# Batch 0 of a polysketch attention + tanh-shrink FFN kernel: token-major on TensorE instead of transposed on VectorE

## The chip, the cores and the metric

The kernel runs on one core of one Trainium2 chip. The metric is the device time of one execution in microseconds (us). Before the change it is 114.63 us, the median of three runs (113.7, 114.63, 115.8).

## What is computed

Two stages are chained. The attention takes 4 batches of 4 heads, 1088 tokens of 32 numbers each:

```python
def phi(x):                                   # S1, S2: 8 x 32
    a = np.einsum('rd,bhsd->bhsr', S1, x)
    b = np.einsum('rd,bhsd->bhsr', S2, x)
    return np.einsum('bhsi,bhsj->bhsij', a, b).reshape(*x.shape[:-1], 64)
q_p, k_p = phi(q), phi(k)
kv  = np.einsum('bhsf,bhsd->bhfd', k_p, v)    # 64 x 32 per head
z   = np.sum(k_p, axis=2)
num = np.einsum('bhsf,bhfd->bhsd', q_p, kv)
den = np.einsum('bhsf,bhf->bhs', q_p, z)[..., None] + 1e-06
attn = num / den
```

Its result, as x with 4352 tokens (4 x 1088) of 128 numbers (4 heads x 32), goes through a feed-forward stage (FFN) of width 2048:

```python
h = x @ w_in              # 4352 x 2048
g = h - np.tanh(h)
out = g @ w_out           # 4352 x 128
```

The kernel computes h W_out as x (W_in W_out): one 128 x 128 product, kept as a high and a low bf16 part (`wch`, `wcl`). So the FFN is, per group of columns (tokens), 16 matmuls h = W_in^T x, 16 tanh with a minus sign, 16 matmuls with W_out, and two with `wch` and `wcl`.

## The kernel before, in words

All work is recorded as operations with inputs and outputs (`P.add`), and a planner in the kernel (`_Prog.schedule`, L151) decides at build time in what order each engine gets them, by costs written beside each operation (`_v`, `_a`, `_pe`, ...) and keys (due times). What runs on the chip are five fixed queues, one for each engine, with semaphore waits between them. Each engine works its queue strictly in order.

**Attention, per batch.** k and q are loaded with (head, time slot) on the partitions, VectorE turns them in 32 x 32 blocks (`kT` L583, `qT` L592), TensorE applies the sketch matrices (`ksk` L599/L610, `qsk` L724), and VectorE turns the result from PSUM back to token-major (`abk` L616, `abc` L729). For k, VectorE multiplies out the 64 products per token (`w`, L659, three pieces), and TensorE sums them against v (`kvmm`, L671); the result, values by features, is spread by ScalarE (`kvd`), turned on TensorE (`kvt`, L703) and copied (`kvb`). The denominator comes from a small Gram matrix of k's two sketches (`gram` L638, `scmm` L625). For q, VectorE forms the denominators (`m`, `den`, `rd`, `ap`, L741 to L749), the products (`qp`, L767) and turns them (`qpT`, L772); TensorE makes the numerators (`num`, L783, 32 x 32 tiles), and ScalarE and VectorE copy them to `xT` (x transposed, bf16, columns are tokens). Batch 0 is cut in pieces of 2, 3 and 4 blocks of 128 tokens, so that the FFN can start on the first 256 columns.

**FFN.** Ten groups of columns: 256, 384, 448, six of 512, and 192 (`GCOLS`). `h` is L877, the tanh `th` is L881 on ScalarE, the second product is L892 and L896. From group 7 on (`PAIRS`) a tanh covers two PSUM banks. VectorE turns each finished group (`ot`, L901), and SyncE writes it out (L911).

**Weights.** ScalarE and GpSimd cast W_in and W_out to bf16; TensorE turns W_in (`wit`, L845), ScalarE copies it (`wiT`), and 16 matmuls (`wc`, L855) make the 128 x 128 product.

**Loads.** All by SyncE's queue, in the order k0, the first 8 slots of q0, v0, one quarter of W_in, the rest of q0, the rest of W_in, W_out, then batches 1 to 3. A load waits (`after`) until no more than `CAP` = 1.4 MB of loads are under way. W_out is fetched in pieces of 512 bytes.

**Fillers.** While TensorE has nothing to do before the first W_out matmul, the planner puts in matmuls on zeros (L435).

Of the kernel before, what the change touches and what calls it, by code (L numbers as in the profile page):

```python
# [22 lines left out]
CAP = 1.4e6  # L23
# [68 lines left out]
class _Prog:  # L92
# [58 lines left out]
    def schedule(self, filler=None):  # L151
# [31 lines left out]
        while n < len(self.ops):  # L183
# [42 lines left out]
            occ, o.lat = o.engs[e]  # L226
            if o.dma:
                free[e] = t + occ
                wire = max(t + 1450.0, wire) + o.dma
                o.t1 = wire + (300.0 if o.key < -79000 else 2000.0)  # L230
            else:
                o.t1 = t + occ
                free[e] = o.t1
# [17 lines left out]
    def fill(self, filler, a, b):  # L251
        t = a
        while t + FILL[0] + FILL[1] < b:
            o = _Op()
            o.engs = {"tensor": (FILL[0], 215.0)}
            o.fn, o.key, o.dma, o.name, o.mode = filler[0], 0, 0, "fill", "128x128"
            o.deps, o.users, o.vals = {filler[1]: True}, [], []
            o.filler = True
            o.eng, o.t0, o.t1, o.lat = "tensor", t, t + FILL[0], 215.0
            o.inc, o.sem, o.waits, o.known = False, None, [], {}  # L260
            o.seq = len(self.order["tensor"])
            self.order["tensor"].append(o)
            t = o.t1
# [58 lines left out]
def _v(n):  # L322
    return {"vector": (n / 0.96 + 64.0, 143.0)}
# [22 lines left out]
def bass_polysketch_attn__then__act_tanh_shrink_kernel(  # L346
# [13 lines left out]
    def sb(name, shape, dtype=FP32):  # L360
        uid[0] += 1
        return nc.alloc_sbuf_tensor(f"{name}_{uid[0]}", shape, dtype).ap()
# [27 lines left out]
    kL = [sb("kL", [128, NC * 32]) for _ in range(B)]  # L390
    vL = [sb("vL", [128, H, NB * 32]) for _ in range(B)]
    qL = [sb("qL", [128, NC * 32]) for _ in range(B)]
    kT_p = pool("kT", 2, [128, 36 * 32])
    qTs = [sb("qT", [128, 36 * 32]) for _ in range(B)]
# [8 lines left out]
    rd_p = pool("rd", 2, [128, NB * H])  # L403
    kvd_p = pool("kvd", 2, [128, 256])
# [4 lines left out]
    NTH = 20  # L409
# [10 lines left out]
    mask4 = sbv("mask4", [128, H])  # L420
    sin = sbv("sin", [128, 2, 32])
# [16 lines left out]
    def pool_op(fn, r=(), w=(), n=100, key=-50000.0):  # L438
# [10 lines left out]
    P.add(_v(128), lambda e, n: e.tensor_reduce(  # L449
        out=mask2.ap[:, :], in_=ident.ap.rearrange("p (a e d) -> p e a d", a=2, e=2), op=ALU.add, axis=AX.XY),  # L450
        r=[ident], w=[mask2], key=-91000)
    for pl, f, val in ((kT_p, lambda a: a[:, 1088:1152], 0.0), 
                       (m_p, lambda a: a[:, :, 8:9], 1e-6)):
        for i, s_ in enumerate(pl.choices):
            o = pool_op(lambda e, n, a=f(s_[1][0]), val=val: e.memset(a, val), n=64, key=-49000)
            pl.seed(i, o)
    qpad = [sbv_ for sbv_ in (_Val(ap=qTs[b][:, 1088:1152]) for b in range(B))]
    for b in range(B):
        pool_op(lambda e, n, b=b: e.memset(qpad[b].ap, 0.0), w=[qpad[b]], n=64, key=-48500 + b)
    vvals = [[_Val(ap=vL[b][e * 64:(e + 1) * 64, :, :]) for e in range(2)] for b in range(B)]  # L460
    for b in range(B):
        P.add(_v(128), lambda e, n, b=b: e.memset(vL[b][64:128, :, 256:288], 0.0), w=[vvals[b][1]], key=-89000 + b)
# [3 lines left out]
    def load(key, o_, i_, w, nbytes, eng="sync", rate=330.0, cap=True):  # L466
        after = []
        if cap:
            left = CAP - nbytes
            for op, nb in reversed(loads):  # L470
                left -= nb
                if left < 0:
                    after = [op]
                    break
        op = P.add({eng: (450.0, 0.0)}, lambda e, n: e.dma_start(out=o_, in_=i_), w=w, key=key, dma=nbytes / rate,
                   after=after)
        loads.append((op, nbytes))
        return op

    for x, Sx in ((0, S1), (1, S2)):  # L480
        load(-99000 + x, sin.ap[:, x, :], Sx[None, :, :].to_broadcast([16, 8, 32]), [sin], 16384, "scalar")

    kvals = [[_Val(ap=kL[b].rearrange("p (r x) -> p r x", r=2)[:, :, e * 288:(544 if e else 288)]) for e in range(2)] for b in range(B)]
    qcut = {0: [0, 8, 34]}
    qvals = [[(a, z, _Val(ap=qL[b][:, a * 32:z * 32])) for a, z in zip(c[:-1], c[1:])]
             for b, c in ((b, qcut.get(b, [0, 34])) for b in range(B))]

    def load_k(key, b):
        src = k[b].rearrange("h (t r c) d -> (h t) r (c d)", r=2, c=17)
        if b == 0:  # L490
            for e in range(2):
                load(key + e, kvals[b][e].ap, src[:, :, e * 288:(544 if e else 288)], [kvals[b][e]], 128 * (256 if e else 288) * 8)
        else:
            load(key, kL[b][:, :], k[b].rearrange("h (t c) d -> (h t) (c d)", c=NC), kvals[b], 128 * 1088 * 4)

    def load_v(key, b):
        vs = v[b].rearrange("h (m x) d -> m h (x d)", x=17)
        for e in range(2):
            w_ = 256 if e else 288
            load(key + e, vL[b][e * 64:(e + 1) * 64, :, 0:w_], vs[:, :, e * 288:e * 288 + w_], [vvals[b][e]], 64 * w_ * 16)  # L500

    def load_q(key, b, i):
        a, z, val = qvals[b][i]
        src = q[b].rearrange("h (t c) d -> (h t) (c d)", c=NC)
        load(key, qL[b][:, a * 32:z * 32], src[:, a * 32:z * 32], [val], 128 * (z - a) * 128)
# [3 lines left out]
    wos = moe_w_out.rearrange("(jb ji) c -> ji jb c", jb=NJB, ji=128)  # L509
# [4 lines left out]
    def load_wo(key, i):  # L514
        load(key, wof[i].ap, wos[:, i * 4:(i + 1) * 4, :], [wof[i]], 128 * 2048)

    lk = iter(range(-90000, -80000, 10))
    load_k(next(lk), 0)
    load_q(next(lk), 0, 0)
    load_v(next(lk), 0)  # L520
    load_wi(next(lk), 0)
    load_q(next(lk), 0, 1)
# [4 lines left out]
    for b in range(1, B):  # L527
        load_k(next(lk), b)
        load_q(next(lk), b, 0)
        load_v(next(lk), b)  # L530

# [6 lines left out]
    def col_time(c):  # L538
# [14 lines left out]
        r=[stt, mask2], w=[wab], key=-85000)  # L553
    for w, z in zip(wqc, wqs):
        pool_op(lambda e, n, z=z: e.memset(z[:, 24:32], 0.0), w=[w], n=8, key=-48600)
        pool_op(lambda e, n, w=w: e.tensor_copy(
            w.ap.rearrange("p (x i) -> p x i", i=8), stt.ap.rearrange("p x (r i) -> p x r i", i=8)[:, :, 0, :]),
            r=[stt], w=[w], n=16, key=-48000)
# [19 lines left out]
    qTv = [[(NC, 36, qpad[b])] for b in range(B)]  # L578
# [9 lines left out]
    def q_transpose(b, i):  # L588
        a, z, val = qvals[b][i]
        tv = _Val(ap=qTs[b][:, a * 32:z * 32])  # L590
        qTv[b].append((a, z, tv))
        P.add(_v((z - a) * 32), lambda e, n: e.transpose(tv.ap, val.ap), r=[val], w=[tv], key=nk(), name=f"qT{b}.{i}")  # L592
# [28 lines left out]
    pg = [_Val(att1 if b else one(2)) for b in range(B)]  # L621
# [43 lines left out]
    pv = [_Val(att1 if b else one(1)) for b in range(B)]  # L665
# [44 lines left out]
    def q_in(b, s0, s1):  # L710
        return [v_ for (a, z, v_) in qTv[b] if a < s1 * 4 and z > s0 * 4]

    def qv4(b):
        return qTs[b].rearrange("p (k g t) -> p k g t", g=4, t=32)

    def q_sketch(b, s0, s1, abc):
# [10 lines left out]
        P.add(_pe(max(sn / 1.2, 55.0) * 2), sk, r=q_in(b, s0, s1) + [scv[b], wqc[b % 2]], w=pq, key=nk(), mode="32x32",  # L727
# [6 lines left out]
    def part(abc, x, c0, c1):  # L734
        return abc.ap.rearrange("p k h f -> p (k h) f")[:, c0 * 4:c1 * 4, x * 8:(x + 1) * 8]

    def q_divide(b, s0, s1, abc):
        nb = s1 - s0
# [3 lines left out]
            out=m_.ap[:, 0:nx, 0:8], in0=part(abc, 0, 0, nb), in1=part(abc, 2, 0, nb),  # L742
# [7 lines left out]
            out=aq.ap[:, 0:nx * 8].rearrange("p (x i) -> p x i", i=8), in0=part(abc, 0, 0, nb),  # L750
# [59 lines left out]

    def attention():
        bias[0] = -15000.0
        k_transposes(0)
        q_transpose(0, 0)
        k_sketch(0)
        gram(0)
        for p in range(3):
            k_outer(0, p)
        kv_mm(0)
        kv_tail(0)  # L820
        st = q_front(0, 0, 2)
        q_piece(0, 0, 0, 2, *st)
        bias[0] = 0.0
        q_transpose(0, 1)
        st = q_front(0, 2, 9)
        for b0, b1 in PIECES[0][1:]:
            q_piece(0, 2, b0, b1, *st)
        for b in range(1, B):
            k_side(b)
            q_transpose(b, 0)  # L830
            st = q_front(b, 0, 9)
            for b0, b1 in PIECES[b]:
                q_piece(b, 0, b0, b1, *st)

    def weights():
        for i in range(4):
            P.add({**_as(512), **_g(512)}, lambda e, n, i=i: copy(e, n, wi[i].ap[:, :], wif[i].ap), r=[wif[i]], w=[wi[i]], key=-1000 + i, name=f"wi{i}")
# [3 lines left out]
        for i in range(2):  # L841
            tp = _Val(bank_h)
            for j in range(8):
# [4 lines left out]
                    r=[wi[jb // 4], identb], w=[tp], key=T_FIRST + 1000 + 4000 * i, mode="128x128", name=f"wit{jb}")  # L848
            P.add(_a(1024), lambda e, n, tp=tp, i=i: copy(
                e, n, wiT[i].ap.rearrange("p j c -> p (j c)"), tp.ap.bitcast(BF16)[:, 0:1024]),  # L850
                r=[tp], w=[wiT[i]], key=T_FIRST + 1000 + 4000 * i, name=f"wiT{i}")
        wc = _Val(bank_h)
        prev = None
        for jb in range(16):
# [3 lines left out]
                key=T_FIRST + 6000, chain=prev, mode="128x128",  # L858
# [5 lines left out]
    def ffn(gi, c0, n_):  # L864
# [38 lines left out]
        ce = (c0 + n_) // 32  # L903
        while cb < ce:
# [86 lines left out]
```

## Time and profile before

| | |
|---|---|
| median of three runs | 114.63 us |
| the profiled execution's own time | 114.65 us |
| its span, first to last instruction | 112.6 us |
| TensorE (PE) busy | 100.3 us, 89% |
| ScalarE (ACT) busy | 79.9 us, 71% |
| VectorE (DVE) busy | 72.1 us, 64% |
| GpSimd (POOL) busy | 5.6 us, 5% |
| first FFN matmul, first tanh | 19.71 us, 20.03 us |
| last `num` of the attention | 82.04 us |
| last tanh ends | 108.46 us |

The profile's times are microseconds from the span's start. PEld is the loading of a matmul's stationary operand, which the profile lists apart from the matmul. A float32 matmul appears as two records for each instruction, a float32 transpose and a bf16 matmul as one. A matmul's listed duration contains its way through the array, so that the distance between starts says more on pace than the duration. "[1.22 <-DMA ...]" behind an instruction is how long its engine had been idle before it and what ended that.

### The profile page before, as it was taken

The page shows a single profiled execution, that of the slowest core. Times are in us where ns is not written, and L with a number is a line of the kernel's source. Part 1 is how long each engine was busy: PE and PEld are TensorE (multiplying, and loading weights), DVE is VectorE, ACT ScalarE, POOL GpSimd, SP SyncE. Part 2 cuts the span into 40 slices and gives each one's busy share as a digit, 9 for nine tenths or more (in the row PEclk, how much of TensorE's full clock was granted, in tenths as well). Part 3 has the DMA queues.
Part 4 walks back from the last instruction along what each step waited for, and adds up shares of the span by engine and source line. Part 5 has one row for each costly group of instructions (what it writes and reads, how often), then busy time and mean ns, then how long its engine had stood idle before and what let it go on. Part 6 is the DMA issues. An engine that isn't in the chain of part 4 may idle for free.

```text
span 112.6 us, 3409 instructions
## 1 busy us (share of the span) xinstructions
PE 100.3 (89%) x1467; PEld 48.7 (43%) x1477; DVE 72.1 (64%) x115; ACT 79.9 (71%) x164; POOL 5.6 (5%) x25
## 2 busy tenths in 40 slices
PE   6975996998799989979999999979999999999960
PEld 4523783455355444436443346334243334334540
DVE  4469374899999999999999992499950020020030
ACT  2101247876487798586599867798969999999950
POOL 5202016000000000000000000000000000000000
PEclk9999999999999999999999999999999999999999
DMA  1999878799987804022000230005004106005035
GB/s 21 259 245 329 255 232 234 243 241 272 226 270 218 165 5 69 0 47 46 0 6 0 44 49 6 6 11 83 0 6 68 25 0 93 0 12 77 4 55 73
DMA packets 25037, 11.24 MB, mean 100 GB/s; under 512 B 18880, under 2 KB 23616, under 8 KB 25024
## 3 DMA queue, kind: packets, MB, share of 16 engines
q1 hardware_dynamic: 24320, 10.97, 40.7%
q8 instruction: 11, 0.18, 0.7%
q10 hardware_dynamic: 704, 0.08, 0.5%
q14 instruction: 2, 0.02, 0.1%
HBM read 8.81 MB, written 2.23 MB: 98 GB/s over the span
## 4 chain that ended last, share of the span: by engine, by line
PE 36%; ACT 28%; DVE 16%; DMA 13%; issue 2%; SPq 1%; DVEq 0%
ACT th L881 25%; PE psb L892 11%; PE psb L877 10%; DMA qL<-in_q_dram 5%; DMA wo_f<-in_moe_w_out_dram 5%; PE psb L783 5%; DVE qp L767 4%; DVE qpT L772 4%; DVE abc L729 3%; DMA kL<-in_k_dram 3%; PE psb L724 3%; PE psb L671 3%; DVE ot L901 2%; PE psb L610 2%; ACT wiT L375 2%
## 5 line engine op out<-in xcount | busy, mean ns | idle before, releaser
L881 ACT ACTIVATE th<-psb 128x512 bf16<-128x512 f32 (+4 forms) x136 | 69.5, 624 | 7.4 <-PE psb L877 6.6
L877 PE MATMUL psb<-xT,wi 128*128 128x512 bf16 (+4 forms) x155 | 50.1, 349 | 1.5 <-DVE xT L375 0.5
L892 PE MATMUL psb<-th,wo 128*128 128x512 bf16 (+4 forms) x157 | 48.2, 348 | 1.4 <-DVE ot L901 0.6
L877 PEld LDWEIGHTS psb<-xT,wi 128*128 128x128 bf16 x160 | 14.9, 97 | 25.3 <-ACT th L881 14.4
L892 PEld LDWEIGHTS psb<-th,wo 128*128 128x128 bf16 x160 | 14.6, 97 | 15.7 <-ACT th L881 7.5
L901 DVE STREAM_TRANSPOSE ot<-psb 128x512 f32<-128x512 f32 (+4 forms) x10 | 6.3, 626 | 22.6 <-PE psb L892 22.6
L772 DVE STREAM_TRANSPOSE qpT<-qp 128x768 f32<-128x768 f32 (+1 forms) x14 | 12.1, 861 | 0.4
L767 DVE TENSOR_TENSOR qp<-ap,abc 128x768 f32<-128x768 f32 (+1 forms) x14 | 11.5, 818 | 0.1
L659 DVE TENSOR_TENSOR w<-abk 128x768 f32<-128x768 f32 x12 | 11.3, 981 | 0.1
L729 DVE STREAM_TRANSPOSE abc<-psb 128x1152 f32<-128x1152 f32 (+2 forms) x5 | 5.7, 1143 | 5.1 <-PE psb L724 5.0
L435 PE MATMUL psb<-zz 128*128 128x256 bf16 x33 | 7.8, 388 | 1.1 <-DVE zz L434 1.1
L783 PE MATMUL psb<-qpT,kvb 32*32 32x128 f32 (+4 forms) x448 | 8.3, 309 | 0.1
L375 ACT CAST xT<-psb 128x192 bf16<-128x192 f32 (+4 forms) x8 | 3.3, 421 | 5.4 <-PE psb L783 5.4
L583 DVE STREAM_TRANSPOSE kT<-kL 128x576 f32<-128x576 f32 (+1 forms) x8 | 5.6, 724 | 1.7 <-DMA kL<-in_k_dram 1.7
L783 PEld LDWEIGHTS psb<-qpT,kvb 32*32 32x32 f32 x448 | 5.1, 103 | 2.9 <-DVE qpT L772 2.0
L671 PE MATMUL psb<-w,vL 128*32 128x64 f32 x288 | 6.0, 243 | 0.0
L592 DVE STREAM_TRANSPOSE qT<-qL 128x1088 f32<-128x1088 f32 (+2 forms) x5 | 5.3, 1055 | 0.9 <-DMA qL<-in_q_dram 0.9
L435 PEld LDWEIGHTS psb<-zz 128*128 128x128 bf16 x33 | 4.1, 135 | 3.6 <-DVE zz L434 1.1
L671 PEld LDWEIGHTS psb<-w,vL 128*32 128x32 f32 x288 | 5.1, 125 | 0.3 <-issue 0.2
L642 ACT COPY gm<-psb 128x32 f32<-128x32 f32 x4 | 0.8, 198 | 5.6 <-PE psb L638 5.6
L724 PE MATMUL psb<-qT,wq 32*32 32x288 f32 (+2 forms) x160 | 3.6, 381 | 0.9 <-ACT xT L375 0.9
L375 DVE CAST xT<-psb 128x192 bf16<-128x192 f32 (+3 forms) x6 | 2.8, 467 | 1.1 <-PE psb L783 1.0
(55 smaller groups left out, 56.6 us busy)
## 6 DMA issues: line engine op xcount, KB each, us to landing
kL<-in_k_dram SPq DMA_DIRECT2D x3, 544.0 KB, 3.6
qL<-in_q_dram SPq DMA_DIRECT2D x3, 544.0 KB, 4.9
vL<-in_v_dram SPq DMA_DIRECT2D x4, 288.0 KB, 4.8
vL<-in_v_dram SPq DMA_DIRECT2D x4, 256.0 KB, 5.0
wi_f<-in_moe_w_in_dram SPq DMA_DIRECT2D x4, 256.0 KB, 4.7
wo_f<-in_moe_w_out_dram SPq DMA_DIRECT2D x4, 256.0 KB, 5.8
out_dram<-ot SPq DMA_DIRECT2D x16, 64.0 KB, 2.0
out_dram<-ot SPq DMA_DIRECT2D x8, 56.0 KB, 1.9
```

The lines of the kernel that those rows point to most:

```text
L375: return e.copy(o, i) if name == "scalar" else e.tensor_copy(o, i)
L435: filler = (lambda e, n: e.matmul(bank(3)[:, 0:256], zz.ap[:, 0:128], zz.ap[:, 128:384], start=True, stop=True), zop)
L659: P.add(_v(768), lambda e, n: e.tensor_tensor(out=wv.ap.rearrange("p (x i j) -> p x i j", i=8, j=8), in0=abh(0)[:, :, :, None].to_broadcas ...
L671: i = e.matmul(pv[b].ap[h * 32:(h + 1) * 32, 0:64], vL[b][:, h, blk * 32:(blk + 1) * 32], wvs[b, p].ap[:, (bi * 4 + h) * 64:(bi * 4 + h + ...
L729: P.add(_vp(sn * 4), lambda e, n: e.transpose(abc.ap.rearrange("p k h f -> p h k f")[:, :, 0:s1 - s0, :], psa4[:, :, 0:sn].rearrange("p h ...
L767: P.add(_v(cn * 256), lambda e, n, qp=qp, c0=c0, cn=cn: e.tensor_tensor(out=qp.ap[:, 0:cn * 256].rearrange("p (x i j) -> p x i j", i=8, j= ...
L772: P.add(_v(cn * 256), lambda e, n, qp=qp, o0=o0, cn=cn: e.transpose(qt.ap[:, o0 * 256:(o0 + cn) * 256], qp.ap[:, 0:cn * 256]), r=[qp], w=[ ...
L783: i = e.matmul(psa4[h * 32:(h + 1) * 32, g, 0:nb * 32], kvb.ap[g * 32:(g + 1) * 32, x, h * 32:(h + 1) * 32], qq[g * 32:(g + 1) * 32, 0:nb, ...
L877: P.add(_pe(n_ / 2.4 + 2.6), lambda e, n, jb=jb, hv=hv: e.matmul(hv.ap[:, jb % m * 512:jb % m * 512 + n_], wi[jb // 4].ap[:, (jb % 4) * 12 ...
L881: P.add(_a(n_ * m), lambda e, n, hv=hv, th=th: e.activation(out=th.ap.rearrange("p (u x) -> p u x", u=m)[:, :, 0:n_], in_=hv.ap.rearrange( ...
L892: fn = lambda e, n, x=x, st=st, sp_=sp_: e.matmul(ov.ap[:, 0:n_], wo[x // 4].ap[:, x % 4, :], ths[x][0].ap[:, ths[x][1] * 512:ths[x][1] * ...
L901: P.add(_vp(n_), lambda e, n: e.transpose(ot.ap[:, 0:n_], ov.ap[:, 0:n_]), r=[ov], w=[ot], key=-60000, name=f"ot{gi}")
```

## The change

The first batch is done another way; batches 1 to 3 keep the old way.

- k0, q0 and v0 are loaded token-major: token 8p+j (for q: 2p+j or 3p+j within a piece) on partition p, all heads beside each other; the last 64 tokens in a small load of their own. Nine loads in place of six, with pieces of 512 bytes (k), 256, 384 and 128 bytes (q) and 1 KB (v). All of q0 is now ahead of W_in.
- k and q are turned on TensorE: for each block of 128 tokens four matmuls against the identity, one per head, each 32 rows high (`transposes0`); the PSUM result is copied by ScalarE (VectorE for the one small piece).
- The sketches are matmuls with the turned block as the 128 x 128 stationary operand and a block-diagonal matrix `wqd` as the moving one (64 columns for k, 96 for q with the denominator's 8 columns per head), so that their result is token-major already; ScalarE copies it out of PSUM.
- `kvmm` becomes 18 matmuls with the products `w` as stationary operand (two heads, 128 features) and v as the moving one: the result is features by values, and goes to a block-diagonal `kvb0` in four small copies. `kvd`, `kvt` and `kvb` of batch 0 go.
- q's products are turned by TensorE transposes of 128 x 128 (18 of them) and copied by ScalarE and VectorE; `num` is a 128 x 64 matmul per head pair.
- W_out is viewed as rows of 2 KB (`(i p j) c -> p i j c`); W_in's cast reorders its columns to match.
- The load cap is 2.6 MB for batch 0 and the weights, 1.4 MB after. Batch 3 reuses the buffers of batch 0, and the th ring grows from 20 to 36 slots of 512.
- The planner's numbers change (DMA latency and rate, TensorE at half pace up to `WARM`, keys of W_in's turning). One of the two `wiT` copies moves to VectorE.
- Output of batch 0's groups is written by other strides, with four more small DMAs for the last 64 rows.

```diff
-CAP = 1.4e6
+CAPS = (2.6e6, 1.4e6)
+WARM = 6300.0
+WKEY = (300.0, 300.0, 1500.0)
...
-    NTH = 20
+    NTH = 36
...
-    wos = moe_w_out.rearrange("(jb ji) c -> ji jb c", jb=NJB, ji=128)
+    wos = moe_w_out.rearrange("(i p j) c -> p i j c", i=4, j=4)
...
+    def transposes0(src, srcv, dst, j0, j1, pool, name):
+        n_ = (j1 - j0) * 128 - (64 if j1 == 9 else 0)
+        pt = _Val(pool)
+        for j in range(j0, j1):
+            kk = 64 if j == 8 else 128
+            def tr(e, n, j=j, kk=kk):
+                for h in range(H):
+                    i = e.matmul(pt.ap[h * 32:(h + 1) * 32, (j - j0) * 128:(j - j0) * 128 + kk],
+                                 src[0:kk, h, j * 32:(j + 1) * 32], ident.ap[0:kk, 0:kk], start=True, stop=True)
+                return i
...
+                P.add(_pe(112), lambda e, n, j=j, j0=j0, pk=pk: e.matmul(
+                    pk.ap[:, (j - j0) * 64:(j - j0 + 1) * 64], kT0.ap[:, j * 128:(j + 1) * 128],
+                    wqd[:, :, 0:16].rearrange("p h (x i) -> p x h i", x=2), start=True, stop=True),
...
+        def kvm(p):
+            for blk in range(p * 3, p * 3 + 3):
+                def f(e, n, blk=blk):
+                    for pr in range(2):
+                        bi = blk % 3
+                        i = e.matmul(pvv[pr].ap[:, 0:64], ws[p].ap[:, (bi * 2 + pr) * 128:(bi * 2 + pr + 1) * 128],
+                                     vL[0][:, pr * 2:pr * 2 + 2, blk * 32:(blk + 1) * 32], start=(blk == 0), stop=(blk == 8),
+                                     skip_group_check=True)
...
+                        P.add(_pe(112), lambda e, n, qp=qp, pr=pr, ci=ci, kk=kk, o0=(c0 + ci - b0) * 128: e.transpose(
+                            pts[pr].ap[:, o0:o0 + kk], qp.ap[0:kk, (ci * 2 + pr) * 128:(ci * 2 + pr + 1) * 128], ident.ap[0:kk, 0:kk]),
...
+                def num(e, n, pn=pn, ja=ja, w_=w_):
+                    for pr in range(2):
+                        i = e.matmul(pn.ap[pr * 64:(pr + 1) * 64, 0:w_], kvb0[:, pr, :],
+                                     qv()[:, pr, ja * 128:ja * 128 + w_], start=True, stop=True)
```

The queues as built: in TensorE's queue the first FFN matmul now stands behind 36 + 36 turning matmuls of k and q, 9 + 9 sketch matmuls, 18 of `kvm`, four of the `qp` transposes, 12 of the 16 `wit` and the first `num`; the other 14 `qp` transposes, two further `num` steps and the last four `wit` follow between the first FFN matmuls. The k sketch of batch 1 stands behind 5 h matmuls (21 before), the last `num` of the attention behind 2432 columns' worth of h matmuls (2752 before). In ScalarE's queue the cast of W_out's second quarter and the copies of `kvb0` and `qpT` stand ahead of the first `xT` copies.

## Prediction

> **What bounds the kernel now.** I read the chain of waits first, then busy time by windows, then the timeline of the first 20 us. The chain, start and length in us:
>
> ```profile
> 1.48 3.58 DMA kL<-in_k_dram
> 5.08 5.62 DMA qL<-in_q_dram
> 10.71 5.61 DMA wo_f<-in_moe_w_out_dram
> 16.34 0.62 ACT wo L375
> 16.96 1.83 ACT wiT L375 x2
> 18.79 0.18 ACT xT L375
> ...
> 84.43 20.98 ACT th L881 x28
> ```
>
> Up to 18.97 us everything leads to the first xT: loads, then a W_out cast and two wiT copies that stand ahead of an xT copy in ScalarE's queue. At the end tanh runs without a gap. Between, the windows (PE, PEld, DVE, ACT and POOL busy us, then granted clock, DMA share, GB/s):
>
> ```profile
> 20.00:25.00 5.00, 4.85 (x68) 2.22 (x67) 4.79 (x8) 4.53 (x16) 0.00 (x0) 1.00 0.87 239
> 25.00:30.00 5.00, 4.09 (x147) 2.60 (x119) 4.93 (x10) 2.89 (x8) 0.00 (x0) 1.00 0.88 258
> 40.00:50.00 10.00, 8.82 (x117) 3.87 (x116) 9.73 (x17) 7.52 (x18) 0.00 (x0) 1.00 0.17 27
> 70.00:84.00 14.00, 13.20 (x145) 4.96 (x146) 10.71 (x15) 12.03 (x25) 0.00 (x0) 1.00 0.13 21
> 84.00:106.00 22.00, 21.75 (x102) 8.53 (x103) 1.81 (x3) 21.89 (x31) 0.00 (x0) 1.00 0.24 36
> ```
>
> TensorE and VectorE are both nearly full from 20 to 70 us, ScalarE is full only after 84. So three things set the end: when the first h starts (19.71 us), how well TensorE is filled until the attention is over, and ScalarE's pace after. The timeline shows TensorE's own pace:
>
> ```profile
> 1.12 4.24 PE L435 MATMUL psb<-zz 128*128 128x256 bf16 x19 [1.12 <-DVE zz L434]
> 10.73 1.51 PE L671 MATMUL psb<-w,vL 128*32 128x64 f32 x48
> 14.80 1.59 PE L845 MATMUL psb<-identb,wi 128*128 128x128 bf16 x13
> 35.03 1.19 PE L671 MATMUL psb<-w,vL 128*32 128x64 f32 x72
> 36.97 0.38 PE L703 MATMUL psb<-ident,kvd 128*128 128x128 f32 x2
> ```
>
> 48 records of L671 took 1.51 us at 10.73, 72 took 1.19 at 35.03: early on TensorE works at half pace, though the granted clock reads 1.00. The 13 wit matmuls are still 122 ns apart at 15 us; full pace comes at about 16.2. 4.24 us of fillers did not bring it. Nearly gapless work from 10.5 to 16.2, 5.7 us, did.
>
> **Start: batch 0's work up to the first h.** VectorE loses kT (0.78+0.70), the first qT (0.45), abk (0.85), abc (0.45) and qpT (0.71) from this path; TensorE gets their work. The path begins as before with k: its first 288 KB landed at 4.2 us (kT started then); for 256 KB in 512-byte pieces I take 4.4.
>
> TensorE's work from there to h, at full pace:
> - Turning k and q: 72 instructions, 144 records, in tiles 32 wide. The nearest row is L671, the same tile with 64 columns: 1.03 us from its first record to the next instruction over 72 records, 14.3 ns each. Here a record has 128 columns; by records 14.3 ns, by columns 28.6. I take the middle, 21.5: 3.1 us (bounds 2.1 and 4.1).
> - k sketch, q sketch, kvm: 36 instructions, 72 records with a full 128 x 128 float32 operand to load. The nearest row is L703, 128 columns: its two records hold TensorE for 0.22 us, 110 ns each, load included. For 64 to 96 columns that gives 55 ns if the columns pace (82 for q's 96), 110 if the load does. L671's loads last 110 ns each and pace nothing, so I let the columns pace: 54 x 55 + 18 x 82 ns = 4.4 us (bounds 4.4 and 7.9).
> - Four qp transposes at 0.11: 0.44. Twelve wit at 0.056 (eight L855 start to end in 0.62, their pace 0.056): 0.67. First num, 8 records of 128 columns, two at a time: 0.44. Gram and scmm by their rows 0.30 + 0.18. Seven fillers at 0.108 (half the early 0.223): 0.75.
>
> Sum 10.3 us, lower end 9.3, upper end 14.8. The half pace goes on until 4.24 to 5.7 us of unbroken work are done, so from 4.4 to about 9.4 (8.6 to 10.1): half of 4.7 us is lost, 2.35. Waits that TensorE can't fill: the copies kc and abk before the sketches, gm, scmm, sc before q's sketch, about 1.0 (0.3 if TensorE is late itself); at the end the qpT copy 0.38, two xT copies of 0.28 and the hops, 1.6 in all, of which wit and fillers cover 1.0: 0.6. First h: 4.4 + 10.3 + 2.35 + 1.0 + 0.6 = 18.7 us, 1.0 earlier than 19.71.
>
> Loads: nine issues in place of six. Early ones took 0.60 to 0.83 us each, so all nine are out by 7 to 8 us and W_in follows without a wait on the 1.4 MB cap. DMA was saturated already (share 1.02 from 5 to 10 us, 271 GB/s), so the higher cap only removes the short waits of SyncE. W_out's quarters land at 15 to 17 us, ahead of the xT copies at about 17.8; the ACT cast ahead of these then costs nothing. If they came at 18, h would slip by 0.5.
>
> The Trainium skill states in "TensorE: Matmul & The Clock Gate", LDWEIGHTS, that a load takes its columns over 1.2 GHz, 107 ns for 128, and under Weight-path perf modes that float32 gets no fast load. That speaks against the change: by it the 72 records would be paced by loads, 7.7 us in place of 4.4. L671's overlapped loads are only 32 wide, so no row here decides it.
>
> In "DMA: Bandwidth & Descriptors", Specifications, the skill states that pieces below 512 B miss the line rate; q0's have 256, 384 and 128. No large load in this trace has pieces that small, so nothing here shows it.
>
> **After the first h.** Before, 92.9 us lie between h and the span's end. What changes:
> - TensorE, added: 14 qp transposes at 0.11 (1.55), num of 832 columns in two tiles at 0.83 ns a column and record (1.4), four wit (0.25); removed: the two num steps of 0.96 and 1.07. Net +1.2, on the path as TensorE is full.
> - ScalarE, added 2.2 us of copies (one of 384, two of 448, xT of 256, 128, 64 columns, less 0.69): hidden, as ScalarE has 15 us of gaps between 20 and 84.
> - VectorE is done with batch 0 earlier: kT of batch 1 started at 27.73, now about 22. The attention runs some 320 columns ahead of the FFN. Gone are waits of TensorE for VectorE: 0.9 in 25 to 30 us, and in 47.5 to 49.3 us (xT and qp late) 1.3: -2.2.
> - Those 320 columns move behind the attention's end, where ScalarE paces: 16 tanh of 0.50 make 8.0 us per 512 against TensorE's 34 x 0.216 = 7.3; 0.7 x 320/512 = +0.45.
> - The wiT copy on VectorE (1.0) falls before batch 1's w products, which have the 5 us of lead; nothing. If the lead is gone, +1.0.
> - SyncE: the batch 3 loads now wait for TensorE's last read of batch 0, and v3 stands behind the first output; v was wanted at 68 us before, so nothing. Four more output DMAs: nothing.
>
> Net -0.55; bounds -2.0 (new order fits all through) to +1.65 (nothing of the 2.2 is recovered).
>
> Likeliest time: the profiled execution's own 114.65 (span 112.6 and 2.05 around it; the median of the runs is 114.63, so no correction) - 1.0 - 0.55 = 113.1 us.
>
> **Rivals.**
> 1. *TensorE becomes the bound of batch 0: slower.* Its records pace at the upper ends: +3.5 for loads, +1.0 for the turning, +0.35 as the half pace then lasts to 10.1, less 0.7 of waits then filled; h at 22.85, time 117.25. For: nothing idles on TensorE in that stretch to absorb it, and the half pace doubles all that comes before 9.4. Against: L671's free loads. It decides (over 2% slower, 116.9) from h at 22.5. If the half pace lasts to 16.2 as before, 118 to 119.
> 2. *The lead is worth nothing*, because TensorE is full anyway (9.91 of 10 from 30 to 40): h at 18.7 but +1.65 after: 115.3, no change. That is also where the change does not do what it says for loads: DMA share was 1.0 already.
> 3. *It fits better than the sum*: turning at 14.3 ns (-1.0), h at 17.7, and -2.0 after: 110.65.
>
> **How the numbers follow.** Two per cent, about what a measurement of this kernel can tell from no change, is 2.3 us: below 112.3 is faster, above 116.9 slower. Likeliest case together with rival 3, 0.62: 110.2 to 114.7 round 113.1, 0.36 of it below 112.3 as the unknown order effects reach to -2.0, 0.26 above. Rival 2: 0.13, no change. Rival 1: 0.25, slower, nearly all of it. Faster 0.36, same 0.39, slower 0.25. The likeliest case's own range is 110.2 to 114.7; for 8 in 10 the range has to take in the near half of rival 1: 110.2 to 117.3.
>
> **What would show it.** First h between 17.5 and 20; distance between the records of the sketches and kvm 55 ns (110: rival 1); wit matmuls 56 ns apart by then (122: half pace stayed); kT of batch 1 on VectorE near 22; no gap of TensorE before group 3's h; tanh without a gap from the last num on, some 5 us longer than before. I am wrong if h starts before 17 or after 22, or if TensorE has new waits of over 2 us in 20 to 80 us.

## The result and the profile after

The changed kernel takes 117.83 us (median of 4 runs, 117.31 to 118.19) against 114.19 us of the kernel before beside it (113.7 to 115.8). The ratio is 1.033, with a 95% interval from 1.025 to 1.041: slower. The prediction was 113.1 us, with 110.2 to 117.3 as its range. The profiled execution took 117.31 us, its span is 115.2 us. Some executions of a kernel run a per cent or more longer than its others; the ratios leave these out, the medians take in all executions.

The chain of waits (start us, length us, what):

```profile
1.12 2.95 PE psb L448 x13
4.07 2.37 PE psb L870 x72
6.45 2.15 PE psb L890 x18
...
12.55 1.73 PE psb L929 x14
14.28 3.99 PE psb L955 x36
18.27 0.46 PE psb L998 x4
18.75 0.42 DVE qpT L382
19.18 0.54 DVE ap L796
19.74 2.63 DVE qp L990 x2
22.41 0.66 PE psb L998 x4
```

Before, the way to the first h led through loads, a cast and copies; now it is TensorE without a gap from 1.12 to 18.7 us (fillers at its start and between its steps included): turning (L870), sketches (L890, L929), kv sum (L955). Then VectorE takes 2.63 us for two qp products that took 0.97 + 0.59 in the chain of before. GpSimd casts W_in and W_out beside VectorE. Its two casts of W_in before:

```profile
9.70 0.76 POOL L375 CAST wi<-wi_f 128x512 bf16<-128x512 f32 x1 [4.16 <-DMA wi_f<-in_moe_w_in_dram]
13.81 0.61 POOL L375 CAST wi<-wi_f 128x512 bf16<-128x512 f32 x1 [3.35 <-DMA wi_f<-in_moe_w_in_dram]
```

GpSimd's and ScalarE's casts after:

```profile
12.84 7.26 POOL L382 CAST wi<-wi_f 128x512 bf16<-128x512 f32 x3 [7.30 <-DMA wi_f<-in_moe_w_in_dram]
19.69 3.14 POOL L382 CAST wo<-wo_f 128x512 bf16<-128x512 f32 x3
14.83 2.48 ACT L382 CAST wi<-wi_f 128x512 bf16<-128x512 f32 x1
```

VectorE's work in the same stretch, after, and below it the `ap` and `m` of before:

```profile
12.64 0.20 DVE L794 RECIPROCAL rd<-den 128x8 f32<-128x8 f32 x1
12.88 1.87 DVE L796 TENSOR_TENSOR ap<-abc,rd 128x64 f32<-128x64 f32 x1
14.79 0.69 DVE L990 TENSOR_TENSOR qp<-ap,abc 128x512 f32<-128x512 f32 x1
15.39 2.02 DVE L788 TENSOR_TENSOR m<-abc 128x224 f32<-128x224 f32 x1
17.45 0.42 DVE L791 TENSOR_REDUCE den<-m 128x28 f32<-128x252 f32 x1
17.90 0.33 DVE L794 RECIPROCAL rd<-den 128x28 f32<-128x28 f32 x1
```

```profile
14.12 0.38 DVE L749 TENSOR_TENSOR ap<-abc,rd 128x64 f32<-128x64 f32 x1
21.09 0.39 DVE L741 TENSOR_TENSOR m<-abc 128x224 f32<-128x224 f32 x1
```

A W_in cast took GpSimd 0.61 to 0.76 us before; now three follow each other at 2.4 us each (7.26 / 3), 2.46 to 2.91 us from start to end. ScalarE's took 0.62 before and 2.48 now. The cast reads W_in with a step of 16 bytes, so as to put its columns in the order that W_out's 2 KB rows ask for. VectorE's `ap` and `m`, 0.38 and 0.39 us before, took 1.87 and 2.02.

The windows (PE, PEld, DVE, ACT, POOL, then granted clock, DMA share, GB/s) answer to those of before:

```profile
20.00:25.00 5.00, 4.13 (x35) 2.76 (x33) 4.71 (x6) 3.45 (x10) 2.83 (x4) 1.00 0.86 243
25.00:30.00 5.00, 4.90 (x75) 3.08 (x76) 4.02 (x7) 3.39 (x13) 0.00 (x0) 1.00 0.86 233
40.00:50.00 10.00, 9.88 (x240) 4.87 (x238) 9.84 (x15) 8.12 (x22) 0.00 (x0) 1.00 0.35 72
70.00:84.00 14.00, 13.47 (x114) 4.88 (x115) 9.19 (x13) 12.40 (x26) 0.00 (x0) 1.00 0.13 20
84.00:106.00 22.00, 21.90 (x98) 8.16 (x99) 2.15 (x3) 21.96 (x32) 0.00 (x0) 1.00 0.23 36
```

TensorE's waits for VectorE did go (40 to 50 us: 9.88 busy against 8.82), but from 20 to 25 it has a new one. The first h stands at 20.40 us (19.71 before), the last `num` at 79.03 (82.04). So the attention is over 3.0 us earlier, and ScalarE's tanh still end later. What lies behind the last `num` has grown: from the last `num` to the span's end 36.2 us against 30.6.

In what follows, two numbers are read from each profile: the start of the first h, and the stretch from there to the span's end. Before they are 19.71 and 92.9 us, after 20.40 and 94.8. The change lost 0.7 us before the first h and 1.9 behind it. These two profiles lie 2.6 us apart, the medians 3.6; what the other 1.0 us is, one profile of each kernel can't tell.

### The profile page after: what moved, and what is told of

The parts are those of the page before. It is cut to its first block, busy times and chain, and to the rows that moved or that the text cites. A ratio compares the mean times of both kernels' runs of the same rounds, so it can differ in the third digit from the quotient of the medians.

```text
span 115.2 us, 3235 instructions
## 1 busy us (share of the span) xinstructions
PE 107.0 (93%) x1368; PEld 56.1 (49%) x1376; DVE 69.6 (60%) x107; ACT 86.9 (75%) x180; POOL 12.4 (11%) x26
## 4 chain that ended last, share of the span: by engine, by line
PE 65%; ACT 26%; DVE 4%; issue 1%
ACT th L1095 26%; PE psb L1106 16%; PE psb L1091 15%; PE psb L830 4%; PE psb L870 4%; PE psb L955 3%; PE psb L448 3%; PE psb L718 3%; PE psb L768 2%; DVE qp L990 2%; PE psb L929 2%; PE psb L890 2%; PE psb L998 2%; PE psb L657 2%; PE psb L1110 2%; PE psb L1014 1%
## 5 line engine op out<-in xcount | busy, mean ns | idle before, releaser
L382 POOL CAST wi<-wi_f 128x512 bf16<-128x512 f32 x3 | 7.3, 2697 | 7.3 <-DMA wi_f<-in_moe_w_in_dram 7.3
L382 ACT CAST xT<-psb 128x128 bf16<-128x128 f32 (+5 forms) x12 | 4.0, 370 | 4.3 <-PE psb L830 3.1
L830 PE MATMUL psb<-qpT,kvb 32*32 32x288 f32 (+2 forms) x256 | 5.5, 352 | 0.0
L448 PE MATMUL psb<-zz 128*128 128x256 bf16 x20 | 4.4, 369 | 1.1 <-DVE zz L447 1.1
L773 DVE STREAM_TRANSPOSE abc<-psb 128x1152 f32<-128x1152 f32 x3 | 4.1, 1379 | 1.7 <-PE psb L768 1.7
L955 PE MATMUL psb<-vL,w 128*128 128x64 f32 x36 | 4.2, 274 | 0.0
L955 PEld LDWEIGHTS psb<-vL,w 128*128 128x128 f32 x36 | 4.1, 192 | 0.0
L990 DVE TENSOR_TENSOR qp<-ap,abc 128x512 f32<-128x512 f32 (+1 forms) x4 | 4.0, 1015 | 0.1
L788 DVE TENSOR_TENSOR m<-abc 128x288 f32<-128x288 f32 (+2 forms) x5 | 3.6, 723 | 0.5 <-ACT abc L382 0.4
L796 DVE TENSOR_TENSOR ap<-abc,rd 128x288 f32<-128x288 f32 (+2 forms) x5 | 3.8, 763 | 0.1
```

The source lines that it names most:

```text
L382: return e.copy(o, i) if name == "scalar" else e.tensor_copy(o, i)
L448: filler = (lambda e, n: e.matmul(bank(3)[:, 0:256], zz.ap[:, 0:128], zz.ap[:, 128:384], start=True, stop=True), zop)
L830: i = e.matmul(psa4[h * 32:(h + 1) * 32, g, 0:nb * 32], kvb.ap[g * 32:(g + 1) * 32, x, h * 32:(h + 1) * 32], qq[g * 32:(g + 1) * 32, 0:nb, ...
L955: i = e.matmul(pvv[pr].ap[:, 0:64], ws[p].ap[:, (bi * 2 + pr) * 128:(bi * 2 + pr + 1) * 128], vL[0][:, pr * 2:pr * 2 + 2, blk * 32:(blk + ...
L990: P.add(_v(cn * 256), lambda e, n, qp=qp, c0=c0, cn=cn: e.tensor_tensor(out=qp.ap[:, 0:cn * 256].rearrange("p (x i j) -> p x i j", i=8, j= ...
```

## Experiments

Three theories. **1:** the W_in casts with a step of 16 bytes are slow and block VectorE. **2:** TensorE is the bound of batch 0, by its float32 loads of 128 columns. **3:** behind the first h TensorE is full, so what the change added to it there pushes the tanh back. All medians below stand beside runs of the kernel before of 113.8 to 114.0 us.

**W_out in 512-byte rows, W_in straight.**

```diff
-    wos = moe_w_out.rearrange("(i p j) c -> p i j c", i=4, j=4)
+    wos = moe_w_out.rearrange("(jb ji) c -> ji jb c", jb=NJB, ji=128)
...
-                e, n, wi[i].ap.rearrange("p (j f) -> p f j", j=4), wif[i].ap.rearrange("p (f j) -> p f j", j=4)), ...
+                e, n, wi[i].ap[:, :], wif[i].ap), ...
```

> The changed kernel with W_out in 512-byte rows again and W_in cast straight through; the order of all instructions is the same. Theory 1 (the strided W_in casts hold GpSimd and ScalarE four times as long and slow VectorE beside them): each W_in cast takes 0.6 to 0.8 us instead of 2.4 to 2.7, the VectorE steps at 12.9 and 15.4 us take 0.4 instead of 1.9 to 2.0, first h between 19.6 and 20.3, and the first five h are followed without the stop behind the qp of 19.7 us; time 115.8 to 116.8, that is 1.0 to 2.0 below the changed kernel. Theory 2 (TensorE alone is the bound of batch 0, by its float32 loads): first h stays at 20.2 to 20.5, time 117.2 to 118. If the 2 KB rows were worth something as loads, W_out lands later and wo casts move behind 17 us.

116.18 us, ratio to before 1.017 (1.008 to 1.026). First h 20.82, stretch 93.1 us. Three of the four W_in casts are back at 0.6 us; the one that runs beside VectorE's third `w` product takes 1.17.

**2 KB rows kept, reordering in TensorE's stationary operand** (the `wit` matmuls alike).

```diff
-  hv.ap[...], wi[jb // 4].ap[:, (jb % 4) * 128:(jb % 4 + 1) * 128], xt, ...
+  hv.ap[...], wi[jb // 4].ap.rearrange("p (f j) -> p j f", j=4)[:, jb % 4, :], xt, ...
```

> The changed kernel with the 2 KB rows kept and W_in cast straight through; the reordering of W_in's columns is done where TensorE reads them, as a stationary operand with a step of 8 bytes, in the h and wit matmuls. Theory 1: as in the run with plain rows, 1.0 to 2.0 us below the changed kernel, if the strided load costs TensorE nothing; if it does, h matmuls show more than 0.216 us each and the time rises by up to 136 h times the difference. Theory 2: 117.2 to 118.

116.1 us, ratio 1.018 (1.011 to 1.025). First h 20.04, stretch 93.9. The strided loads of h last 113 ns instead of 96 and pace nothing. Both runs agree, and their ratios stand 0.015 to 0.016 below the changed kernel's 1.033: the slow casts cost about 1.7 us, and rows of 2 KB in themselves bring nothing. That theory 2 is the only cause ("117.2 to 118") has fallen. Most of the gain lies behind the first h: in the profiles the stretch is 1.7 us shorter in the first run and 0.9 in this one, and TensorE is busy for all 5 us from 20 to 25 in both, 4.13 in the changed kernel. That the first run's first h came at 20.82 and not before 20.3 is TensorE's half pace, which lasted longer in that execution (its first 72 turnings took 2.90 us, those of the changed kernel 2.37, those of this run 2.13).

**The kernel before with only the 2 KB rows and the reordering cast.**

```diff
+    wos = moe_w_out.rearrange("(i p j) c -> p i j c", i=4, j=4)
...
+                e, n, wi[i].ap.rearrange("p (j f) -> p f j", j=4), wif[i].ap.rearrange("p (f j) -> p f j", j=4)), ...
```

> The kernel before with only the 2 KB rows of W_out and the W_in cast that reorders columns for them; the order of instructions is that of before. Theory 1: the casts of W_in take 2.4 to 2.7 us each here too, VectorE slows beside them, and wit and the first xT come later: first h at 20.5 to 22.5, time 115.5 to 117.5. Theory 2: the casts hide in GpSimd's idle time, first h within 0.4 of 19.7, time 114.2 to 114.9.

116.81 us, ratio 1.023 (1.015 to 1.030). First h 21.90, stretch 92.9, as before. So this one part, alone, costs the old kernel 2.6 us (0.0228 x 113.93). There the first `wit` stands ahead of the kv sum in TensorE's queue, and waits for the cast:

```profile
11.96 0.29 PE L846 MATMUL psb<-identb,wi 128*128 128x128 bf16 x1 [3.29 <-POOL wi L375]
12.20 1.51 PE L671 MATMUL psb<-w,vL 128*32 128x64 f32 x48
```

The same wait was 1.24 us before. Part of the loss comes through TensorE's clock: after its longer waits the profile grants it 0.50 from 19 to 21 us, where it worked at full pace before.

**All reordering casts on ScalarE** (changed kernel, `_g(512)` dropped from the W_in cast's engines).

> The changed kernel with all four reordering W_in casts on ScalarE and none on GpSimd. Theory 1 has two halves: the cast is slow in itself, and VectorE is slow while GpSimd casts. If the second half is true, VectorE's 64-column ap takes 0.2 to 0.4 us and the 224-column m 0.4 to 0.5, instead of 1.87 and 2.02 in the changed kernel; if VectorE was slow for another reason, they stay near 2. ScalarE then holds 10 us of casts ahead of batch 0's copies, so first h comes at 21.5 to 23 and the time is 118 to 120.

One execution: 121.92 us, later than expected, first h 24.98. ScalarE held 9.5 us of casts ahead of batch 0's copies, and TensorE, waiting for it, was granted a clock of 0.67 from 20 to 25 us and 0.65 from 25 to 30. VectorE answers the question:

```profile
12.91 0.22 DVE L796 TENSOR_TENSOR ap<-abc,rd 128x64 f32<-128x64 f32 x1
13.17 0.69 DVE L990 TENSOR_TENSOR qp<-ap,abc 128x512 f32<-128x512 f32 x1
14.78 0.39 DVE L788 TENSOR_TENSOR m<-abc 128x224 f32<-128x224 f32 x1 [0.92 <-ACT abc L382]
```

0.22 and 0.39 us: it was GpSimd's slow cast that held VectorE. GpSimd is idle up to 14.28 us here, and the `m` at 14.78 runs beside its straight casts of W_out. Both halves of theory 1 stand.

**Twelve of the 18 kv matmuls left out**, in the changed kernel with its slow casts.

```diff
+                    if blk % 4:
+                        return e.matmul(pvv[0].ap[0:32, 0:64], ws[p].ap[:, 0:32], vL[0][:, 0:2, blk * 32:(blk + 1) * 32], ...)
```

> The changed kernel with 12 of the 18 kv matmuls of batch 0 left out (only three of nine blocks are summed, a 32-wide placeholder matmul stands for each other block), so kv of batch 0 lacks most of its sum. It takes about 2.3 to 2.6 us of TensorE's work out of the path to the first h. Theory 2 (TensorE is the bound there): first h at 17.9 to 18.4, time 115.2 to 115.9. Theory 1 (VectorE, slowed by the strided casts beside it, is just as late: its m, den and rd end at 18.2 ahead of the kv copies): first h no earlier than 19.7, time within 0.8 of the changed kernel.

116.78 to 119.7 us, ratio 1.028 (1.016 to 1.040) against the changed kernel's 1.033: no gain that can be told from none. The profile is of the longest execution, 119.7 us, in which the granted clock fell to 0.50 from 20 to 25 us, so its first h (23.05) proves little. It does show VectorE in the way: the last `w` product of batch 0 took 2.53 us in its chain beside a W_in cast that began earlier (11.56 us), against 0.95 in the changed kernel. By itself this run would have spoken against theory 2; as VectorE, held by GpSimd, stood close behind TensorE, it doesn't decide. So theory 2 had to be tried without the slow casts.

**The kv sum of batch 0 in bfloat16**, on the kernel with the reordering at TensorE's read (its base, and that of the next two runs). The bfloat16 copy of v takes the room of two slots of the th ring.

```diff
-                out=ws[p].ap.rearrange("p (x i j) -> p x i j", i=8, j=8),
+                out=ws[p].ap.bitcast(BF16)[:, 0:768].rearrange("p (x i j) -> p x i j", i=8, j=8),
...
-                        i = e.matmul(..., ws[p].ap[:, ...], vL[0][:, pr * 2:pr * 2 + 2, ...], ...)
+                        i = e.matmul(..., ws[p].ap.bitcast(BF16)[:, ...], vb.ap[:, pr * 2:pr * 2 + 2, ...], ...)
```

> The kernel of the run with the reordering at TensorE's read (2 KB rows, W_in cast straight through), and batch 0's kv sum in bfloat16: VectorE writes the products as bfloat16, GpSimd casts v once (1152 columns). 36 float32 records at 111 ns (3.99 us) become 18 at about 56 ns, the pace of the wit records (1.0 us). Theory 2 (TensorE is the bound of batch 0): first h 2.5 to 3.0 us earlier than 20.0, that is 17.0 to 17.5, time 113.0 to 113.8, below that of its base (116.1) by as much. Rival (VectorE or the W_out cast ahead of the xT copy on ScalarE is next, no more than 1 us behind TensorE): first h at 18.7 to 19.2, time 114.9 to 115.4.

113.7 us, 2.4 below its base; ratio 0.997 (0.994 to 1.001). The chain of its base, then its own:

```profile
14.04 3.99 PE psb L955 x36
18.04 0.45 PE psb L998 x4
```

```profile
15.48 0.52 PE psb L956 x18
16.06 0.63 PE psb L1000 x4
```

From the first kv matmul to the first h it takes 2.77 us (18.25 - 15.48) against 6.00 (20.04 - 14.04). That is 3.2 us, a little more than expected; the median gains 2.4. The first h itself, 18.25, lies between the two expected ranges, since in the profiled execution the half pace lasted 1.44 us longer (3.57 against 2.13 us for the first 72 turnings); whether it did in the others isn't known. The time speaks for theory 2: TensorE's work on batch 0 is the bound up to the first h.

**Each of the 14 later qp turnings done twice** (`for _ in range(2 if b0 else 1)` round the transpose), on the same base.

> The kernel of the run with the reordering at TensorE's read, with each of the 14 turnings of q products behind the first h done twice: 1.5 to 2.2 us of TensorE's work more, between 20 and 25 us, same order. Theory 3 (TensorE is full until the attention is over): time 117.6 to 118.5, that is 1.5 to 2.4 above its base. Rival (TensorE's work there hides beside VectorE's, or beside ScalarE's tail): 116.0 to 116.6.

117.12 us, 1.0 above its base, between theory 3's range and the rival's. The turnings themselves took 3.6 us in the chain (2.35 + 1.27) against 2.2, so 1.4 more, and the stretch is 94.7 against 93.9: in this profile a little over half of the added work reaches the end. Theory 3 is half right.

**q products, their turning and num in bfloat16**, first with the kv sum left in float32, then with both.

```diff
-                            pts[pr].ap[:, o0:o0 + kk], qp.ap[0:kk, ...], ident.ap[0:kk, 0:kk]),
+                            pts[pr].ap.bitcast(BF16)[:, o0:o0 + kk], qp.ap.bitcast(BF16)[0:kk, ...], identb.ap[0:kk, 0:kk]),
```

> The kernel of the run with the reordering at TensorE's read, with only batch 0's q products, their turning and num in bfloat16; the kv sum stays float32. It takes about 0.5 us of TensorE's work from the path to the first h and about 2 us from 20 to 26 us behind it. Theory 3 (TensorE is full behind the first h): 113.8 to 114.8, that is 1.3 to 2.3 below its base (116.1). Rival (only what lies before h counts; behind it VectorE, the loads or ScalarE are as late): 115.3 to 115.9.

114.69 us, 1.4 below its base; the ratios, 1.004 (1.000 to 1.007) against 1.018, make it 1.7. First h 19.76, stretch 92.3 against 93.9: 0.3 us before the first h, 1.6 behind it. The saving behind h is real, and within theory 3's range.

> The run before this one, and batch 0's q products, their turning by matmul and the num matmuls in bfloat16 as well: 18 turnings at about 56 ns instead of 110 to 157, num with one record in place of two. Of this some 0.5 us of TensorE's work lies before the first h and 1.7 to 2.2 us behind it. Theory 3 (TensorE is full until the attention is over, so what the change added to it behind the first h pushes the tanh back): 1.5 to 2.5 us below the kernel with bfloat16 in the kv sum alone. Rival (the added work hides beside VectorE): no more than 0.6 below it.

111.82 us, ratio 0.973 (0.962 to 0.985): 1.5 to 3.8% below the kernel before. The median moved as expected (1.9 below the run with the kv sum alone; 2.7 by the ratios), but the profile, of one of the longer executions (112.03 us), doesn't give theory 3's reason: first h 16.28, stretch 93.7, no shorter than with the kv sum alone (93.4). From 30 to 40 us TensorE is busy for only 8.36 us. The chain shows what had become late there, batch 2's loads one behind the other, and its `qT`:

```profile
18.53 3.82 DMA vL<-in_v_dram
22.37 7.50 DMA qL<-in_q_dram
29.90 1.31 DVE qT L640
```

**The caps.** On the float32 kernel with the reordering at TensorE's read, 1.4 MB for all loads (`CAPS = (1.4e6, 1.4e6)`):

> The kernel of the run with the reordering at TensorE's read, with 1.4 MB of loads in flight instead of 2.6 MB; order unchanged. If the higher cap only removes short waits of SyncE: W_in and W_out land within 0.5 us of where they did, time 115.8 to 116.4. If the loads' lead is worth something, as the change's name says: W_in lands 1 us later or more, time 116.8 or more.

116.04 us, first h 20.01, W_in casts from 11.6 us on instead of 12.15. So the 2.6 MB in flight bring nothing that can be told. On the bfloat16 kernel, whose attention is far enough ahead to want its loads, `CAPS = (2.6e6, 2.6e6)`:

> The kernel with batch 0's kv sum, q products and num in bfloat16, and 2.6 MB of loads in flight for all loads, not only for the first; only the place of one output among SyncE's issues differs. In its base batch 2's q was issued at 22.4 us behind the 1.4 MB cap and landed at 29.9, and TensorE was busy for 8.36 of the 10 us from 30 to 40. If that wait is what keeps the saved TensorE work from showing behind the first h: q lands by 27, TensorE busy over 9.7 of 10 there, time 0.8 to 1.6 below the base (111.8), 110.2 to 111.0. Rival (VectorE or the tail's ScalarE is as late): within 0.4 of 111.8.

112.45 to 116.54 us, too scattered to compare. q came in time (`qT` at 28.86 without a wait), but the stretch is 93.8, no shorter than its base's 93.7. In TensorE's timeline stands a new stop inside one group of matmuls, with nothing in the profile that releases it:

```profile
29.21 0.71 PE L658 MATMUL psb<-kT,wab 64*32 64x288 f32 x14
31.42 0.64 PE L658 MATMUL psb<-kT,wab 64*32 64x288 f32 x2 [1.50 <-issue]
```

So the load had been late, and in this profile what its earlier arrival gave was lost again. Two packets of the queue that the profile calls "instruction" fall into the stop (30 to 31 us). A late fetch of instructions is thus a candidate for it, not tried; the base has two such packets from 26 to 28 us without a stop. Between the two, `CAPS = (2.6e6, 1.8e6)`:

> The kernel with batch 0's kv sum, q products and num in bfloat16, and 1.8 MB of later loads in flight, between the 1.4 MB with which batch 2's q came at 29.9 us and the 2.6 MB with which q came in time but TensorE stood still for 1.5 us behind nothing that the profile shows, at a DMA share of 1.05. If the standstill comes from the crowded DMA: none of over 0.5 us with share below 1.0 from 25 to 32, q before 28.5, time 110.3 to 111.6. If not: 112 or more.

110.99 us (110.47 to 111.6), ratio 0.973 (0.969 to 0.977): 2.7% faster than the kernel before. q was turned at 28.34 us, the stop at the same place is 0.41 us, and the stretch is 92.4. But the ratio is that of 1.4 MB, 0.973, so no gain from the cap is shown by the times. And the DMA share was 1.05 from 25 to 30 us, not below 1.0 as I had asked of a small stop, so that the crowded DMA causes it is not shown.

## Why the prediction was wrong

**A step was missing: the reordering cast.** The text before the prediction says that W_in's cast reorders its columns; the prediction gave the casts of W_out nothing and did not price that of W_in at all. It cost about 1.7 us of the 3.6, taken back by two different edits; put on the old kernel it costs 2.6. No row of before shows a cast that reads with a step, so a bound from both sides was owed for it, and for what GpSimd does to VectorE beside it. This is the step that failed in kind: a cost that the sum held at nothing.

**A step was mis-decided: "I let the columns pace".** For the 72 records of sketches and kv sum the prediction had 4.4 us, with 7.9 as its upper bound by loads, and named the Trainium skill's rule ("TensorE: Matmul & The Clock Gate", LDWEIGHTS) that spoke for loads. They took 2.15 + 2.15 + 3.99 = 8.29 us, above even the upper bound: 111 to 119 ns a record, the kv sum's with 64 columns as long as the 110 of the L703 row with 128. So the columns don't pace them. The rule (107 ns for 128 columns) fits; the row that I followed had operands of 32 columns. Rival 1 named this mechanism and its sign (110 ns between records), and its +1.0 for the turning was near the truth too. That its 117.25 us lies so close to the measured 117.83 is luck all the same: it put the first h at 22.85, where 20.40 was measured, and knew nothing of the casts.

**The sum for the first h**, 18.7 against 20.40 in the profiled execution:
- k landed in time for 4.07, not 4.4: -0.3.
- Turning took 28.7 ns a record where it ran on without a break, the columns' pace, and 4.4 us in all at full pace for k and q instead of 3.1 (upper bound 4.1): +1.3.
- Sketches and kv sum: +3.9.
- Half pace: the first 72 records took 2.37 us where 28.7 ns each give 2.07, so it cost 0.3 and not 2.35 (half of the prediction's own 4.4 to 9.4 would have been 2.5): -2.05. By these numbers it ended at about 4.7 us, an estimate, not at 9.4. The prediction counted the unbroken work from 4.4 us on; here it began with the fillers at 1.12 and ran on into the turning.
- Waits that TensorE can't fill: none, as it was late itself: -1.6.

That gives 19.95; 0.45 is left over and not resolved. Large errors of opposite sign hid each other here: +5.2 us of TensorE's work, -3.65 us of half pace and waits. That the first h came out only 1.7 us late is partly luck.

**Behind the first h**, -0.55 foretold and +1.9 measured, 2.45 apart. The regained waits for VectorE were there (from 20 to 80 us TensorE idles for 1.99 us, 3.96 before), and so was the longer tail (5.6 us; "some 5 us" foretold). `kT` of batch 1 came at 23.35, not 22. The slow casts cost 0.9 to 1.7 of the stretch (93.9 and 93.1 without them). The added TensorE work was mis-sized by 0.95: 2.2 us for the 14 turnings instead of 1.55, 1.7 for num instead of 1.4. The run with q's products in bfloat16 shows what this work is worth, 1.6 us of stretch when about 2 us of it are gone, the doubled turnings 0.8 for 1.4. The prediction had all of it on the path, which is a little too much. Casts and mis-sized work together make up some 1.4 to 2.65 of the 2.45 us, by these numbers; the runs don't divide it further.

**What held, and what the signs missed.** The loads were no bound: W_out's cast stood ahead of xT without cost, and the higher cap brings nothing. But neither sign that I had named for being wrong showed: the first h was inside 17 to 22 us, and TensorE's waits from 20 to 25 us come to 0.87. A loss out of several parts passes such coarse signs. The finer ones did tell: the first h was outside 17.5 to 20, and the sketches and kv sum stood 111 to 119 ns apart, not 55.

## What to carry to other kernels

When a layout is changed for the sake of a transfer, find where the reordering is paid: here a cheaper-looking row cost 1.7 us in a cast, and was free when TensorE read the operand with the step. Moving work from a half-idle engine to one that is nearly full needs its cheapest form there; the same change with batch 0's kv sum, q products and num in bfloat16 beat the kernel before by 2.7%. And price a stationary operand by its own width and type: here a row with 32 columns was off by a factor of two for 128.

## What the runs showed of the hardware

- A 128 x 512 float32 to bfloat16 cast that reads with a step of 16 bytes took 2.5 us on ScalarE and 2.46 to 2.91 on GpSimd, against 0.62 and 0.61 to 0.76 straight in the kernel before. The Trainium skill, "SBUF — State Buffer" (under Door 1: The DMA port swizzle), says that SBUF has lines of 16 bytes and that each access to a new line pays a penalty; four float32 share such a line, and the factor here is about four (2.48 / 0.62 on ScalarE).
- While GpSimd cast, VectorE's steps with two inputs in SBUF (`ap`, `m`, `qp`) stood for up to 2 us, though not each of them (`qp` at 14.79 us took its 0.69); reductions, reciprocals and copies out of PSUM kept their times (`den` 0.42, `rd` 0.33). The same page ("SBUF: two separate sides") states that a GpSimd operation which reads SBUF and a VectorE operation with two inputs in SBUF lock each other out for a whole instruction. Beside a straight cast the wait was shorter: in the run with the reordering at TensorE's read, `qp` of 512 took 1.08 us at 12.90 beside GpSimd's casts and 0.68 at 21.35 without. GpSimd is held as well: in the run with 512-byte rows the straight cast beside VectorE's `w` product took 1.17 us.
- A float32 stationary operand of 128 x 128 paced TensorE at 111 to 119 ns a record with 64 or 96 columns moving; in bfloat16 with 64 columns the pace was 29 ns (18 in 0.52 us).
- TensorE's half pace ended at a different moment from run to run: the first 72 turnings, which follow the same 13 fillers, took 2.13 to 3.57 us. With 28.7 ns a record at full pace and twice that before, it ended between about 4.2 and 7.1 us, an estimate. In the profile of the kernel before, with gaps on TensorE, it lasted to about 16.2 (13 `wit` matmuls 122 ns apart up to there). In both the granted clock reads 1.00; it does show the half pace that came back after a wait (0.50 from 19 to 21 us in the old kernel with the reordering cast).
- TensorE stopped once for 1.50 us with no wait that the profile shows, in a stretch with a DMA share of 1.05; with a smaller cap the stop at the same instruction was 0.41 us. The cause stays open.
